# Zero products of TensorE in the idle spots of a planned attention-and-mixer kernel, with one PSUM bank less for the first batch

## The chip, the cores and the metric

The kernel runs on one core of a Trainium2 chip. The metric is the device time of one execution in microseconds (us). The engines are TensorE (PE in the profile; its weight loads are PEld), VectorE (DVE), ScalarE (ACT), GpSimd (POOL) and SyncE (SP). PE multiplies from SBUF into PSUM, which has eight banks of 512 float32 columns per partition; DVE and ACT read PSUM and work on SBUF.

## The reference

Block-sparse attention over 4 batches, 8 heads, 768 tokens and head size 64, followed by a residual mixer. Every query block of 32 tokens sees its neighbours, the first and the last block, and three sampled ones:

```python
scores = q @ k.T / sqrt(D);  scores = where(mask, scores, -1e9)
attn = softmax(scores);      x = attn @ v            # heads side by side: (4, 768, 512)
a1 = alpha1 * x + beta1
u = x + lam * einsum('ts,bsd->btd', w_tok, a1)       # tokens are mixed
a2 = alpha2 * u + beta2
out = u + lam * (relu(a2 @ w_ch1) @ w_ch2)           # channels, 512 -> 2048 -> 512
```

Inputs and output are float32; the kernel multiplies in bfloat16 and float16.

## The kernel before

Heads are handled in 16 pairs, four pairs to a batch, and each pair in 9 units of 1024 score columns. A unit is a scores job on PE (line 658, or 736 for the later pairs, into one of two PSUM tiles "sps"), an exponential on ACT (line 673 or 762, into one of 11 SBUF tiles "eT"), for the later pairs a masking on DVE (line 767), and a P·V job on PE (line 698, function `single`, for pairs 0 to 5; line 794, function `pv_of`, for the others). The P·V jobs of one head accumulate over four and a half units (or nine half ones) in one PSUM bank; behind the last, `norms` takes the reciprocal of the row sums (line 630) and multiplies (line 633), which frees the bank. When a pair is normalised, DVE prepares its tokens (lines 850, 858), PE multiplies by w_tok (line 870), DVE adds and scales (880, 886), and a transpose (907, for the first batch) brings it to the layout that the channel products want. When all four pairs of a batch are there, the first channel product (line 943) makes 16 tiles for each half batch, which ACT or DVE turn by relu into "hts" (954, 958), and the second (line 988) multiplies these by w2b into a bank "cp" or, late, "ops".

PSUM is full: two tiles "sps" of two banks each, two tiles "mm" of one bank (transposes, token products, first channel products), one bank "ops" and one bank "cp". For batch 0, when no second product exists yet, a head's P·V may take either "ops" or "cp" (line 712).

The order of the work is written by a planner at build time. Every piece of work is a `Job` with an engine, a duration in ns from simple formulas, a priority (a smaller tuple goes first), the jobs that it depends on, and the slots that it takes and gives back. A clock runs through events; whenever an engine is free by its own account, the ready job of the best priority whose slots are free is put next on that engine (from line 1088). Scores have priority 1, P·V and transposes 2, token products 3, and channel products 4 and 5. The jobs are emitted in this order, and `pin_order` (line 49) fixes it for each engine. On the chip nothing is timed: each engine runs its instructions in that order and waits for the semaphores that they need. `st["ch2"]` becomes true when the first second-product job takes "cp"; until then the planner has no channel product with w2b in hand. `pe_idle` lists the stretches in which PE, by the planner's clock, has nothing to do.

Loads are issued on POOL's queue in a fixed order, held back by the planner's estimate of the DMA's backlog and, for later pairs, by a flag that DVE raises at a chosen unit (lines 306, 324). SP's queue issues the stores of the output and the transposing DMAs of the later pairs.

Before the attention begins, products of a zeroed tile are issued on PE, nine of 512 columns and later seven of 128 columns:

```python
    warm = wk.tile([P, 512], BF, name="warm", tag="eT", bufs=NET)
    nc.vector.memset(warm[:], 0.0)
    wps = ps.tile([P, 512], FP, name="cp", tag="cp", bufs=1)

    def keep_warm(n, w):
        for _ in range(n):
            nc.tensor.matmul(wps[:, 0:w], warm[:, 0:P], warm[:, 0:w], start=True, stop=True)
```

They write the bank "cp", which nobody reads before it is overwritten. The tile "warm" is one of the ring of 11 "eT" tiles.

Of the kernel before, what the change touches and what calls it, by code (L numbers as in the profile page):

```python
# [13 lines left out]
BF = mybir.dt.bfloat16  # L14
# [13 lines left out]
P = 128  # L28
# [10 lines left out]
NET = 11  # L39
# [27 lines left out]
def kernel(  # L67
# [41 lines left out]
    pp = ctx.enter_context(tc.tile_pool(name="persist", bufs=1))  # L109
# [51 lines left out]
    for i in range(1, NQB):  # L161
        nc.sync.dma_start(kx[i][MB, :], ind_dr.ap())

    warm = wk.tile([P, 512], BF, name="warm", tag="eT", bufs=NET)
    nc.vector.memset(warm[:], 0.0)
    wps = ps.tile([P, 512], FP, name="cp", tag="cp", bufs=1)

# [475 lines left out]
    def single(p):  # L643
        b, n = pairs[p]
        nonlocal last_pv
        prev_pv = None
        for u in range(NU):
            i = p * NU + u

            def qk(p=p, u=u):  # L650
                sps = ps.tile([P, UN], FP, name="sps", tag="sps", bufs=2)
                f = u * UN
                while f < (u + 1) * UN:
                    a, r = divmod(f, NT * S)
                    jt, c = divmod(r, S)
                    w = min(S - c, 512 - f % 512)
                    h = (2 * p + a) % NQB
                    nc.tensor.matmul(  # L658
                        sps[:, f - u * UN : f - u * UN + w],
                        kx[h][0:KC, ts(jt, P)],  # L660
                        qx[h][0:KC, c : c + w],
                        start=True,
                        stop=True,
                    )
                    f += w
                tl["sps", p, u] = sps
                st["qk"] += 1

            def ex(p=p, u=u):
                eT = wk.tile([P, UN], F16, name="eT", tag="eT", bufs=NET)  # L670
                sps = tl.pop(("sps", p, u))
                for c in (slice(0, 512), slice(512, UN)) if (p, u) == (0, 0) else (slice(0, UN),):
                    nc.scalar.activation(eT[:, c], sps[:, c], AF.Exp, bias=EXPB, scale=SCALE)  # L673
                eTs[p, u] = eT

            hs = {divmod(u * UN, NT * S)[0], divmod((u + 1) * UN - 1, NT * S)[0]}
            deps = [head_ready[2 * p + a] for a in hs]
            if i:
                deps.append(qk_jobs[i - 1])
            give = ("head",) if u in (NU // 2, NU - 1) else ()  # L680
            jq = Job("PE", mmt(2, 512) + (8 if u % 3 != 1 else 8), (1, i), qk, deps, take=("sps",), give=give)
            jq.gate = i
            qk_jobs[i] = jq
            exp_jobs[i] = je = Job("ACT", 950.0, (1, i), ex, [jq], take=("eT",), give=("sps",), lat=160.0)

            lo, hi = u * GU, (u + 1) * GU
            segs = [(lo, hi)] if u != NU // 2 else [(lo, HT), (HT, hi)]
            for si, (s0, s1) in enumerate(segs):
                a = s0 // HT

                def pv(p=p, u=u, s0=s0, s1=s1, a=a):
                    if s0 % HT == 0:
                        tag = tl.pop(("opsel", p, a))
                        ops[p, a] = ps.tile([P, 512], FP, name=tag, tag=tag, bufs=1)
                    vx = vext[p % NV]
                    for i in range(s0, s1):
                        jt, t = divmod(i % HT, NT)
                        nc.tensor.matmul(  # L698
                            ops[p, a][:, t * VW : t * VW + D + 1],
                            eTs[p, u][:, ts(i - u * GU, P)],  # L700
                            vx[:, a, jt, 0 : D + 1],
                            start=(i % HT == 0),
                            stop=(jt == NT - 1),
                            skip_group_check=True,
                        )

                first = s0 % HT == 0
                deps = [je, putv[p]] + ([prev_pv] if prev_pv else [])
                give = ("eT",) if s1 == hi else ()
                if s1 == 2 * HT:  # L710
                    give += ("vext",)
                take = ((("ops", "cp") if b == 0 else ("ops",), ("opsel", p, a)),) if first else ()
                prev_pv = Job("PE", mmt(s1 - s0, D + 1), (2, i, si), pv, deps, take=take, give=give)
                last_pv = prev_pv
                if s1 % HT == 0:
                    pv_last[p, a] = prev_pv
                    norms(p, a)
# [358 lines left out]
    while left:  # L1076
        moved = True
        while moved:
            moved = False
            for e in free_at:  # L1080
                if free_at[e] > t:
                    continue
                best = None
                if e == "POOL" and dma_free[0] - t > AHEAD:
                    seq += 1
                    heapq.heappush(events, (dma_free[0] - AHEAD, -seq, None))
                    continue
                for r, j in by_eng[e]:
                    if r > t or j.done is not None:
                        continue  # L1090
                    if e == "POOL" and j is not loads[0]:
                        continue
                    key = (gated(j), j.prio)
                    if (best is None or key < best[0]) and can(j):
                        best = (key, j)
                if best is None:
                    continue
                j = best[1]
                can(j)
                for tk in j.take:  # L1100
                    if isinstance(tk, tuple):
                        o = chosen[tk[1]]
                        slots[o] -= 1
                        tl[tk[1]] = o
                        tl["slot", tk[1]] = o
                        if o == "cp" and tk[0][0] == "cp":
                            st["ch2"] = True
                    else:
                        slots[tk] -= 1
                j.out = j.fn(e) if len(j.eng) > 1 else j.fn()  # L1110
                if getattr(j, "ch", False):
                    st["ch"] += j.dur
                if e == "PE" and t - free_at[e] > 1:
                    pe_idle.append((free_at[e], t))
                dur = j.alt.get(e, j.dur)
                if getattr(j, "slow", False) and t < 85000.0:
                    dur = 2.2 * dur
                free_at[e] = t + dur
                lat = j.lat if j.lat is not None else DRAIN + SEM if e == "PE" else SEM
                j.done = t + dur + lat  # L1120
                if j.xfer is not None:
                    dma_free[0] = max(dma_free[0], t + 2300.0) + j.xfer
                    j.done = dma_free[0] + 200.0
                    loads.pop(0)
                seq += 1
                heapq.heappush(events, (j.done, seq, j))
                if e == "PE":
                    for s in succ.get(j.n, ()):
                        if s.eng == ("PE",):
                            early.add((j.n, s.n))  # L1130
                            waiting[s.n] -= 1
                            if not waiting[s.n]:
                                by_eng["PE"].append((t + dur, s))
                heapq.heappush(events, (free_at[e], -seq, None))
                for e2 in j.eng:
                    by_eng[e2] = [x for x in by_eng[e2] if x[1] is not j]
                left -= 1
                moved = True
        if not left:
            break  # L1140
        if not events:
            raise RuntimeError(f"stuck at {t}: " + str([(e, len(v)) for e, v in by_eng.items()]) + str(slots))
        t = max(t, events[0][0])
        while events and events[0][0] <= t:
            _, _, j = heapq.heappop(events)
            if j is None:
                continue
            for g in j.give:
                if isinstance(g, tuple):
                    slots[tl.pop(("slot", g))] += 1  # L1150
                else:
                    slots[g] += 1
            for s in succ.get(j.n, ()):
                if (j.n, s.n) in early:
                    continue
                waiting[s.n] -= 1
                if not waiting[s.n]:
                    for e in s.eng:
                        by_eng[e].append((t, s))
# [31 lines left out]
```

## Time and profile before

| | us |
|---|---|
| median of 4 runs | 324.66 |
| lowest and highest | 323.75 and 325.54 |
| profiled execution | 323.75 |
| its span, first to last instruction | 322.0 |
| PE busy | 308.3 |
| DVE busy | 208.9 |
| ACT busy | 206.3 |
| POOL busy | 49.7 |

The mean granted clock of PE over the span is 0.995 of full speed. Busy time of PE counts a product from its start to the end of its drain, and products overlap, so a busy PE isn't PE at its peak. A line such as "L698 MATMUL ops<-vext,eT ... x8" is a group of eight products of line 698 that write the tile ops from vext and eT. In a timeline a row gives the start and the length of such a group, and in brackets how long the engine was idle before it and which instruction's end released it.

### The profile page before, as it was taken

The numbers are of one execution on the slowest core, as the hardware profiler recorded it, in microseconds if no ns is written. First come the engines' busy times: TensorE is split into PE (matmuls) and PEld (weight loads), VectorE is DVE, ScalarE is ACT, GpSimd is POOL, SyncE is SP. The second block draws the span as 40 slices with busy tenths as digits, with TensorE's granted clock in tenths as the row PEclk, the third lists the DMA queues.
The fourth block names the chain that finished last, engine by engine and source line by source line (L and its number), as shares of the span: only waits on it lengthen the run. The fifth ranks groups of instructions, "written<-read, shape, count | busy, mean of one in ns | idle before, by whom it ended". The sixth has DMA issues, their size and how long they took to land.

```text
span 322.0 us, 7616 instructions
## 1 busy us (share of the span) xinstructions
PE 308.3 (96%) x3238; PEld 189.5 (59%) x3238; DVE 208.9 (65%) x416; ACT 206.3 (64%) x262; POOL 49.7 (15%) x77
## 2 busy tenths in 40 slices
PE   7879989899999999999899999999999999999996
PEld 3666868666655465555555455555655565555544
DVE  4559876878987797878778677687778660201001
ACT  4999997897885665746684584756784526354530
POOL 4647132200303030202103030030000000000000
PEclk9999998999999999999999999999999999999999
DMA  6999999996556654073815527064010201201102
GB/s 147 191 236 210 211 239 175 255 156 79 70 79 113 101 101 83 33 126 90 122 26 100 115 53 130 35 105 109 3 26 35 68 24 25 100 0 50 50 22 76
DMA packets 46774, 31.95 MB, mean 99 GB/s; under 512 B 27516, under 2 KB 42264, under 8 KB 46612
## 3 DMA queue, kind: packets, MB, share of 16 engines
q0 software_dynamic: 16496, 17.83, 32.9%
q1 hardware_dynamic: 29992, 13.40, 18.5%
q8 instruction: 25, 0.41, 0.6%
q10 hardware_dynamic: 252, 0.24, 0.3%
q14 instruction: 9, 0.07, 0.1%
HBM read 32.04 MB, written 7.47 MB: 123 GB/s over the span
## 4 chain that ended last, share of the span: by engine, by line
PE 67%; ACT 10%; DVE 7%; issue 6%; DMA 5%; POOL 3%; POOLq 0%; ACTq 0%
PE cp L988 19%; PE mm L943 18%; ACT eT L673 7%; PE ops L794 6%; PE mm L870 6%; PE sps L736 5%; DMA k<-in_k_dram 4%; PE ops L988 4%; PE sps L658 3%; PE sps L943 2%; ACT kx L270 2%; PE ops L698 2%; DMA v<-in_v_dram 2%; PE cp L170 1%; DVE x_sb L880 1%
## 5 line engine op out<-in xcount | busy, mean ns | idle before, releaser
L762 ACT ACTIVATE eT<-sps 128x1024 f16<-128x1024 f32 x90 | 88.1, 1021 | 33.8 <-PE sps L736 32.2
L943 PE MATMUL mm<-uT,w1b 128*128 128x384 bf16 x472 | 90.9, 326 | 0.9 <-DVE x_sb L880 0.5
L954 ACT ACTIVATE hts<-mm,b1t 128x384 bf16<-128x384 f32 x89 | 51.8, 582 | 57.7 <-PE mm L943 55.5
L988 PE MATMUL cp<-w2b,hts 128*128 128x512 bf16 (+1 forms) x336 | 80.1, 374 | 0.7 <-DVE ot L1005 0.7
L943 PEld LDWEIGHTS <-w1b 128*128 128x128 bf16 x512 | 46.7, 97 | 33.4 <-issue 5.0
L767 DVE TENSOR_TENSOR eT<-eT,maskT 128x1024 f16<-128x1024 f16 x90 | 60.6, 685 | 7.7 <-ACT eT L762 7.5
L988 PEld LDWEIGHTS <-hts 128*128 128x128 bf16 x400 | 36.6, 98 | 35.8 <-issue 2.9
L673 ACT ACTIVATE eT<-sps 128x1024 f16<-128x1024 f32 (+1 forms) x55 | 52.6, 1015 | 5.5 <-PE sps L658 5.1
L1005 DVE TENSOR_TENSOR ot<-x_sb,cp 128x512 f32<-128x512 f32 (+1 forms) x21 | 14.1, 672 | 46.2 <-PE cp L988 45.8
L794 PEld LDWEIGHTS <-eT 128*128 128x128 f16 x720 | 29.5, 97 | 18.4 <-DVE eT L767 7.0
L870 PE MATMUL mm<-a1p,wtokT 128*128 128x128 bf16 x576 | 37.1, 221 | 0.1
L794 PE MATMUL ops<-vext,eT 128*128 128x65 f16 x720 | 35.5, 194 | 1.5 <-DVE eT L767 1.5
L658 PE MATMUL sps<-qx,kx 88*128 88x512 bf16 (+1 forms) x144 | 31.7, 329 | 5.3 <-ACT eT L673 4.2
L870 PEld LDWEIGHTS <-wtokT 128*128 128x128 bf16 x576 | 33.6, 99 | 2.5 <-issue 0.5
L736 PE MATMUL sps<-qx,kx 64*128 64x512 bf16 (+1 forms) x240 | 27.3, 326 | 0.0
L306 POOL COPY held<-flag 1x1 bf16<-1x1 bf16 x8 | 5.9, 740 | 131.1 <-DVE flag L324 131.1
L958 DVE TENSOR_SCALAR hts<-mm,b1t 128x384 bf16<-128x384 f32 x29 | 17.8, 615 | 10.7 <-PE mm L943 10.5
L698 PEld LDWEIGHTS <-eT 128*128 128x128 f16 x432 | 19.7, 99 | 5.7 <-issue 0.5
L880 DVE TENSOR_TENSOR x_sb<-x_sb,mm 128x384 f32<-128x384 f32 x32 | 17.6, 550 | 7.3 <-PE mm L870 7.3
L658 PEld LDWEIGHTS <-kx 88*128 88x128 bf16 x144 | 12.8, 98 | 11.4 <-issue 7.0
L886 DVE TENSOR_TENSOR ub<-x_sb,a_bc 128x384 bf16<-128x384 f32 x32 | 17.2, 552 | 0.3
L736 PEld LDWEIGHTS <-kx 64*128 64x128 bf16 x240 | 8.2, 94 | 15.4 <-issue 12.9
(76 smaller groups left out, 238.3 us busy)
## 6 DMA issues: line engine op xcount, KB each, us to landing
out_dram<-ot SPq DMA_DIRECT2D x23, 256.0 KB, 2.0
v<-in_v_dram POOLq DMA_DIRECT2D x16, 192.0 KB, 5.8
q<-in_q_dram POOLq DMA_DIRECT2D x15, 192.0 KB, 3.7
k<-in_k_dram POOLq DMA_DIRECT2D x15, 192.0 KB, 5.1
w1b<-in_moe_w_ch_dram POOLq DMA_DIRECT2D x4, 512.0 KB, 9.9
w2b<-in_moe_w_ch_dram POOLq DMA_DIRECT2D x4, 512.0 KB, 14.9
wtk<-in_moe_w_tok_dram POOLq DMA_DIRECT2D x3, 384.0 KB, 9.7
mask_rows<-maskT POOLq DMA_DIRECT2D x1, 1152.0 KB, 12.8
```

The source lines that it names most:

```text
L658: nc.tensor.matmul(sps[:, f - u * UN : f - u * UN + w], kx[h][0:KC, ts(jt, P)], qx[h][0:KC, c : c + w], start=True, stop=True,)
L673: nc.scalar.activation(eT[:, c], sps[:, c], AF.Exp, bias=EXPB, scale=SCALE)
L698: nc.tensor.matmul(ops[p, a][:, t * VW : t * VW + D + 1], eTs[p, u][:, ts(i - u * GU, P)], vx[:, a, jt, 0 : D + 1], start=(i % HT == 0), s ...
L736: nc.tensor.matmul(sps[:, a * 512 + lo : a * 512 + lo + w], kx[sl][r, ts(jt, P)], qx[sl][r, c : c + w], start=True, stop=True,)
L762: nc.scalar.activation(eT[:], sps[:], AF.Exp, bias=EXPB, scale=SCALE)
L767: nc.vector.tensor_tensor(out=e, in0=e, in1=maskT[:, u, :].unsqueeze(1).broadcast_to([P, 2, 512]), op=ALU.min,)
L794: nc.tensor.matmul(ops[p, a][:, t * VW : t * VW + D + 1], eTs[p, u][:, a * 512 + c * P : a * 512 + (c + 1) * P], vx[:, a, jt, 0 : D + 1], ...
L870: nc.tensor.matmul(tp[:, j, :], wtokT[:, s, ts(3 * g + j, P)], tl["a1p", p][:, s, :], start=(s == 0), stop=(s == NT - 1),)
L880: nc.vector.tensor_tensor(out=sl, in0=sl, in1=tl.pop(("tp", p, g))[:], op=ALU.add)
L943: nc.tensor.matmul(hp[:, 0:HS], w1b[:, dk, ts(f, P)], uTs[b][:, dk, ts(hf, HS)], start=(dk == 0), stop=(dk == 3),)
L954: nc.scalar.activation(hts[kk][:, f, :], hp[:, 0:HS], AF.Relu, bias=b1t[:, f : f + 1], scale=1.0)
L988: nc.tensor.matmul(cps[kk, mi][:, 0:w], hts[kk][:, nk, ts(m, P)], w2tile[0][:, nk, lo : lo + w], start=(nk == 0), stop=(nk == 15),)
```

## The change

Three edits. The tile "warm" gets a buffer of its own, which lives as long as the kernel. The P·V jobs of batch 0 take the bank "ops" alone, as those of the later batches do. And when the planner puts a job on PE while `st["ch2"]` is false, it first emits zero products of 128 columns into the bank "cp": as many as fit into the stretch from PE's planned end of its last job to the start of this one, less 60 ns, at 56 ns each. They are emitted ahead of the job's instructions in PE's order; they take no time on the planner's clock, and nothing waits for them.

```diff
-    warm = wk.tile([P, 512], BF, name="warm", tag="eT", bufs=NET)
+    warm = pp.tile([P, 512], BF, name="warm", tag="warm")
...
-                take = ((("ops", "cp") if b == 0 else ("ops",), ("opsel", p, a)),) if first else ()
+                take = ((("ops",), ("opsel", p, a)),) if first else ()
...
-                j.out = j.fn(e) if len(j.eng) > 1 else j.fn()
                 if getattr(j, "ch", False):
                     st["ch"] += j.dur
+                if e == "PE" and not st["ch2"]:
+                    keep_warm(int((t - free_at[e] - 60.0) / 56.0), P)
+                j.out = j.fn(e) if len(j.eng) > 1 else j.fn()
                 if e == "PE" and t - free_at[e] > 1:
                     pe_idle.append((free_at[e], t))
```

## The prediction

> **What bounds the kernel now.** I read the page first, then busy time by stretch, then the chain of waits and the timeline of the place that they point to. From the page:
>
> ```profile
> PE 308.3 (96%) x3238; PEld 189.5 (59%) x3238; DVE 208.9 (65%) x416; ACT 206.3 (64%) x262; POOL 49.7 (15%) x77
> PE   7879989899999999999899999999999999999996
> ACT  4999997897885665746684584756784526354530
> PEclk9999998999999999999999999999999999999999
> ```
>
> PE is the bound over the whole, but a slice is 8 us, and in the first six or seven ACT is as full as PE while PE has holes. In that stage ACT's exponentials (1015 ns each, line 673) set the pace and PE waits for them; from about 65 us PE is full and sets the end. The only slice whose granted clock is not 9 is the seventh. By stretch (columns: stretch; PE, PEld, DVE, ACT, POOL busy us and count; clock; DMA share; GB/s):
>
> ```profile
> 40.00:44.00 4.00, 3.70 (x70) 3.05 (x68) 3.45 (x7) 3.80 (x5) 3.34 (x5) 1.00 1.27 198
> 44.00:48.00 4.00, 3.10 (x53) 2.50 (x50) 2.42 (x8) 3.95 (x5) 0.00 (x0) 0.86 1.23 274
> 48.00:52.00 4.00, 4.00 (x52) 3.46 (x51) 1.81 (x5) 2.60 (x4) 0.00 (x0) 0.71 1.04 214
> 52.00:56.00 4.00, 4.00 (x77) 3.23 (x75) 3.19 (x8) 3.29 (x5) 1.74 (x3) 1.00 0.87 138
> ```
>
> The clock was granted 0.86 of 4 us and then 0.71 of 4 us. If it was one stretch at half speed, it lasted (0.14 + 0.29) x 4 / 0.5 = 3.4 us; asked alone, 46.8 to 50.3 shows 0.51, so it does. In it ACT, full until then, is busy for 2.60 us of 4: it waits for a slowed PE. What came ahead of it, from PE's timeline (start, length, instruction; in brackets the idle time and who ended it):
>
> ```profile
> 42.87 0.50 PE L212 MATMUL mm<-identb,rel 128*128 128x128 bf16 x6
> 43.67 0.54 PE L454 MATMUL mm<-be2b,w1b 128*128 128x1 bf16 x16 [0.30 <-ACT uT L270]
> 44.59 0.59 PE L658 MATMUL sps<-qx,kx 88*128 88x512 bf16 x3 [0.39 <-ACT eT L673]
> 45.02 0.41 PE L698 MATMUL ops<-vext,eT 128*128 128x65 f16 x8
> 45.41 0.54 PE L454 MATMUL mm<-be2b,w1b 128*128 128x1 bf16 x16
> 46.46 0.64 PE L658 MATMUL sps<-qx,kx 88*128 88x512 bf16 x2 [0.51 <-ACT eT L673]
> ```
>
> Here stand three idle times, and two groups of one-column products that hardly use the array. The printed idle begins when the last product has drained; PE could have issued some 0.14 us earlier (163 ns of a product less the 25 ns between starts, (0.54 - 0.163)/15), so the room at 44.59 is about 0.39 + 0.14 = 0.53 us.
>
> **The change, part by part.**
>
> *Zero products.* How many come in is a count that the code makes: (gap - 60)/56 in each idle spot of the planner's list. For the order of the kernel before, the list holds 119 products in 23 spots up to the first product with w2b (76 us in the trace); the new order will differ somewhat. The duration: the early zero products in the timeline are
>
> ```profile
> 6.25 0.56 PE L170 MATMUL cp<-warm 128*128 128x128 bf16 x7
> ```
>
> so (0.56 - 0.219)/6 = 57 ns from start to start (219 ns is the shortest in the answer on the cp tile). 119 x 57 ns = 6.8 us of issue. They wait for nothing, so what matters is whether each lot fits in the real hole. Worked from starts in the timeline, PE's real holes between 8 and 65 us come to some 9.7 us, and they lie where the planner has them: 9 products (0.51 us) for 0.53 at 44.59; 9 (0.51 us) for 0.51 + 0.14 = 0.65 at 46.46; 17 (0.97 us) for about 0.94 at 58.62. Three lots don't fit: 8 products (0.45 us) ahead of a transpose at 17.54 where there is no hole, 8 (0.45 us) for 0.29 at 32.18, and 7 (0.39 us) ahead of the transpose at 63.65. Behind each lies the next hole (0.52 us at 18.40, 0.22 at 35.53, 0.43 in two holes by 64.43) that PE would have waited out anyway, and this covers the delay. Without that cover the misfits cost 1.07 us in all. I take 0.2 us, range 0 to 1.1. The next job's weight load, which the trace has inside the hole, now follows the zero products; it overlaps the last of them, and its cost is within the 0.2. Two instructions per product add 238 to 7616; the instruction queue carries 0.41 MB in all, 3% more of it is nothing here. No DMA, no POOL or SP instruction is added or moved past.
>
> *The clock.* In the two holes and the one ahead of the first one-column group (3 products) the plan puts 21 products, 1.2 us, in the 3.4 us before the dip. Do zero products count as activity? The answer on the cp tile has the 512-wide zero products at a median of 620 ns against 379 ns for the same width at line 988, and the clock reads 1.00 from 5.9 us on, after nothing but zeros and a handful of small products: so they do. A rule weighs against this. The Trainium skill, "TensorE: Matmul & The Clock Gate", Part 1 and "Why this matters for your kernels", has the clock halved after an idle window of about 3.4 us and advises no gap over some 3 us. The longest idle time here is 0.78 us, so by that rule there is nothing to be dropped and nothing to gain: the sum would be +0.6 us. The row shows a dip of just that length after a sparse, not idle, window, and the row decides. But the same section has the window running freely, not tied to the kernel's start, which no single run can show; then an execution whose windows cut the sparse stretch in two may have no dip, and I keep that as a rival. Value of the dip: at most 3.41 x 0.5 = 1.7 us (PE's lost issue), at least 0 (if the waits behind swallow it). I take the engine that sets the pace in that place, ACT, which lost 4.00 - 2.60 = 1.4 us: -1.4 us.
>
> *One bank less for the first batch.* Heads 1, 3, 5 and 7 of the first batch accumulate in cp, the others in ops. With ops alone, the first P·V job of a head waits for reciprocal and multiply (197 + 557 ns, lines 630 and 633) of the head before. The trace has this already where the second batch begins:
>
> ```profile
> 63.53 0.28 PE L698 MATMUL ops<-vext,eT 128*128 128x65 f16 x4
> 63.65 0.76 PE L907 MATMUL mm<-identb,ub 128*128 128x128 bf16 x6
> 64.43 0.59 PE L658 MATMUL sps<-qx,kx 88*128 88x256 bf16 x3
> 64.86 0.77 PE L698 MATMUL ops<-vext,eT 128*128 128x65 f16 x20
> ```
>
> From 63.65, the last issue of a head, to 64.86 are 1.2 us in which P·V stands still and other work goes on; then it catches up, 20 at a stretch. Behind a waiting P·V job only later P·V jobs queue in the plan, since scores have priority; ACT feels nothing until its 11 eT buffers fill, and 1.2 us is about one exponential. There are seven such turns in the first batch. For the turns near 14, 19, 26, 30 and 42 us a hole of the ACT-bound stage follows, and P·V that was put off goes into it. Those near 36 and 51 us fall in stretches without a hole, where token products (18 x 56 ns) and scores are ready to go first. Only the last head's end leads on: its normalisation at 55.9 to 56.9 us feeds the token product at 59.3, then the first channel product. Bounds: -0.5 (another order may also be luckier) to 7 x 1.2 = 8.4 us if every turn were bare. I take a third of one turn, 0.4 us, by the row above, where other work filled it.
>
> *The warm buffer.* It leaves the eT ring, where it was released by 7 us, and takes 1 KB per partition of its own: 0. What would cover it, the ring of 11, loses nothing.
>
> The sum, against the profiled execution: 323.75 - 1.4 + 0.2 + 0.4 = 322.95 us. That execution (span 322.0 and 1.75 around it) is the fastest of the four shown, 0.91 below their median, so the median to expect is 323.86, say **323.9 us**.
>
> **Rivals.**
>
> *No dip to save* (chance 0.19). The clock dip belongs to the profiled execution and not to the usual one, because the windows fall otherwise. Then +0.6 us stays: 325.3, less if the holes cover the 0.6: 324.7 to 325.3. For it speaks that the execution with the dip is the fastest of four; against it that the sparse stretch from 43.2 to 46.9 is longer than a window.
>
> *The re-sorted plan is worse: slower than before* (0.28). Its one mechanism is the late hand-over from the first batch to the second. P·V is put off in the full stretches at 36 and 51 us and is not made up before the last head's normalisation; then token product, transpose and first channel product come late, and PE, with nothing else ready at 59 to 64 us, idles or issues zeros. Each turn that is not made up costs its 1.2 us less the 0.3 us of one P·V job that was late anyway, 0.9 us. Four of the seven turns (from 30 us on) bare: 3.6 us, with the dip saved or not 325.7 to 328.2; the likeliest here 327. It decides from about 3 us, which outweighs the 1.4 gained and passes 326.3. For it: the page's PE row is 9 in those slices. Against it: the second batch lives with one bank, and the chain of waits names line 633 for only 0.2 us at line 698 and 1.0 us at line 794.
>
> *More than one dip in the usual execution* (0.15). The median lies 0.9 us above the profiled execution; if that is a second dip, the zeros save both: 324.66 - 2.8 + 0.6 = 322.5.
>
> **How the numbers follow.** The likeliest has 0.38, with a range of its own of 322.7 to 325.2 (dip worth 0 to 1.7, misfits to 1.1). All four runs before lie within 0.6%, so 0.5%, 1.6 us, is about what can be told from no change. Faster (under 323.0): the third rival's 0.15 and 0.07 of the likeliest, 0.22. Slower (over 326.3): the re-sorted plan's 0.28 and 0.03 of the others, 0.31. Same: 0.47. The range over the cases: 322.0 to 327.2.
>
> **What the new profile would show.** Right: the row by stretch has 1.00 at 44 to 52 us, ACT is near 4 of 4 there, line 170 has some 130 to 150 products instead of 16, idle times of line 658 from ACT shrink to nearly nothing, and no wait of over 1 us for line 633 stands before 65 us. The first channel product (66.2 us, line 943) comes about 1 us earlier. Wrong: the dip is there again, or elsewhere; or line 943 begins later than 66.2; or the dense part, which should be 255.8 us from there to the end as before, has another length, which would be the order and not the clock.

## The result and the profile after

The changed kernel took 322.21 us (median of 43 runs, 320.73 to 325.67) against 324.3 us for the kernel before (64 runs, 322.32 to 328.01): a ratio of 0.9941, 95% interval 0.9928 to 0.9955. It is 0.6% faster, where the likeliest forecast was 323.9 and "same". (The ratio, here and below, leaves out slow executions, those over 1.5% above the fastest of their kernel, and is not the quotient of the medians.) Its profiled execution has a span of 319.2 us against 322.0. From its page, with the rows shown of before:

```profile
PE 310.4 (97%) x3340; PEld 193.8 (61%) x3340; DVE 206.4 (65%) x411; ACT 208.5 (65%) x267; POOL 48.1 (15%) x77
PE   7999999999999999999899999999999999999996
ACT  4999989897775678756676577746665526254630
PEclk9999999999999999999999999999999999999999
```

PE's holes in the second, third, sixth and eighth slice are filled, and the clock's dip in the seventh is gone. By stretch, with the same columns as before:

```profile
40.00:44.00 4.00, 3.66 (x57) 3.01 (x54) 2.75 (x8) 3.06 (x5) 3.81 (x5) 1.00 1.28 197
44.00:48.00 4.00, 3.83 (x91) 3.33 (x89) 3.28 (x9) 3.98 (x5) 0.02 (x1) 1.00 1.19 272
48.00:52.00 4.00, 4.00 (x72) 3.59 (x69) 3.63 (x11) 3.80 (x5) 0.00 (x0) 1.00 1.00 191
```

ACT is busy for 3.80 of the 4 us from 48 us on (2.60 before). So far the forecast's picture holds. PE's timeline of the place, start and length of each group, shows the zero products (line 170) between the jobs:

```profile
44.64 0.54 PE L454 MATMUL mm<-be2b,w1b 128*128 128x1 bf16 x16
45.04 0.72 PE L170 MATMUL cp<-warm 128*128 128x128 bf16 x10
45.92 0.54 PE L454 MATMUL mm<-be2b,w1b 128*128 128x1 bf16 x16 [0.17 <-DVE kx L272]
46.32 0.27 PE L170 MATMUL cp<-warm 128*128 128x128 bf16 x2
46.43 0.60 PE L658 MATMUL sps<-qx,kx 88*128 88x512 bf16 x2
```

But the first channel product (line 943) begins at 65.5 us instead of 66.2, 0.7 us earlier, and the span is 2.8 us shorter: from there to the end are 253.7 us instead of 255.8. The first start of line 943, before and changed:

```profile
L943 PE MATMUL mm<-uT,w1b x472: 322/326/337, 66.2 to 308.1; 128*128 128x384 bf16 x158
L943 PE MATMUL mm<-uT,w1b x472: 322/326/337, 65.5 to 305.3; 128*128 128x384 bf16 x158
```

In that part neither kernel has zero products or a dip. The prediction had named this sign: another length of the dense part "would be the order and not the clock". One pair of executions is not much for 2 us, but the profiled executions of the experiments below say the same: 253.6 to 255.4 us in nine executions of the new order, 255.8 to 256.3 in three of the old one (and 253.9 in the old one once its late loads are let go, as the last experiment tells).

To see where the time went I set the start of each group of token products (line 870) against its start in the planner's own list; the difference is the lag of the chip behind the plan. The plan's end of PE is 0.75 us earlier in the new order (313.20 against 313.95; these are the planner's figures, not measurements). The lags in us, from the profiled executions (the last three columns are experiments told below):

| token group of | before | changed | bank only, first run | zeros, old order | loads not held |
|---|---|---|---|---|---|
| pair 0, first half | 0.94 | 1.13 | 1.07 | 1.15 | 1.08 |
| pair 3, second half | 2.95 | 1.69 | 2.95 | 1.73 | 2.98 |
| pair 9, second half | 2.25 | 1.76 | 2.59 | 0.71 | 2.14 |
| pair 10, first half | 3.43 | 2.68 | 3.39 | 1.67 | 3.74 |
| pair 11, first half | 4.26 | 2.59 | 3.30 | 2.11 | 3.74 |
| pair 12, first half | 5.13 | 2.74 | 3.63 | 4.38 | 3.56 |
| pair 15, second half | 4.77 | 2.74 | 3.88 | 4.01 | 3.19 |

The span's 2.8 us are thus 0.75 of plan and 2.03 of lag. Of the lag 1.26 is won by pair 3 (the dip), but by pair 9 the kernel before has caught up to within 0.49. Most of the rest comes where it falls back from 3.43 to 5.13 between pairs 10 and 12. The order of PE's jobs differs in 383 of 624 places, from 13 us of the plan to 252; the last 60 us are alike.

Each column is one execution, and the level changes between executions: three of the changed kernel have 2.74, 5.99 and 5.53 in the last row. The growth from pair 10 to pair 12 is what holds. It is 1.70, 2.71 and 2.67 us in three executions of the old order (before, zeros in the old order, and bank of pairs 0 and 1 taken away), and -0.10 to 0.95 us in the nine of the new order (1.26 with twice the zero products).

### The profile page after: what moved, and what is told of

Its sections match the earlier page's. It is cut to its first block, busy times and chain, and to the rows that moved or that the text cites. A ratio compares the mean times of both kernels' runs of the same rounds, so it can differ in the third digit from the quotient of the medians.

```text
span 319.2 us, 7815 instructions
## 1 busy us (share of the span) xinstructions
PE 310.4 (97%) x3340; PEld 193.8 (61%) x3340; DVE 206.4 (65%) x411; ACT 208.5 (65%) x267; POOL 48.1 (15%) x77
## 4 chain that ended last, share of the span: by engine, by line
PE 70%; DMA 14%; DVE 6%; issue 4%; ACT 3%; POOL 3%; POOLq 0%
PE cp L988 20%; PE mm L943 20%; PE ops L794 7%; PE sps L736 6%; DMA q<-in_q_dram 6%; PE mm L870 5%; PE ops L988 4%; DMA mask_rows<-maskT 4%; DMA v<-in_v_dram 3%; PE sps L658 3%; PE cp L170 2%; PE sps L943 2%; DMA k<-in_k_dram 2%; DVE eT L767 1%; DVE hts L958 1%
## 5 line engine op out<-in xcount | busy, mean ns | idle before, releaser
L954 ACT ACTIVATE hts<-mm,b1t 128x384 bf16<-128x384 f32 x96 | 55.9, 582 | 50.8 <-PE mm L943 48.4
L794 PEld LDWEIGHTS <-eT 128*128 128x128 f16 x720 | 29.2, 97 | 17.8 <-issue 4.2
L794 PE MATMUL ops<-vext,eT 128*128 128x65 f16 x720 | 34.8, 194 | 0.3 <-DVE eT L767 0.3
L306 POOL COPY held<-flag 1x1 bf16<-1x1 bf16 x8 | 4.3, 541 | 128.7 <-DVE flag L324 128.7
L698 PEld LDWEIGHTS <-eT 128*128 128x128 f16 x432 | 18.6, 97 | 4.5 <-DVE x_sb L633 0.4
L698 PE MATMUL ops<-vext,eT 128*128 128x65 f16 x432 | 20.5, 193 | 0.0
L958 DVE TENSOR_SCALAR hts<-mm,b1t 128x384 bf16<-128x384 f32 x22 | 13.5, 615 | 8.2 <-PE mm L943 8.2
L633 DVE TENSOR_TENSOR x_sb<-ops,rcp 128x384 f32<-128x384 f32 x32 | 17.8, 557 | 1.1
```

Of the source, the lines that this page charges most:

```text
L633: nc.vector.tensor_tensor(out=x_sb[:, s0 : s0 + NT, h * D : (h + 1) * D], in0=op[:, :, 0:D], in1=rcp[:].unsqueeze(2).broadcast_to([P, NT, D]),
L698: nc.tensor.matmul(ops[p, a][:, t * VW : t * VW + D + 1], eTs[p, u][:, ts(i - u * GU, P)], vx[:, a, jt, 0 : D + 1], start=(i % HT == 0), s ...
L794: nc.tensor.matmul(ops[p, a][:, t * VW : t * VW + D + 1], eTs[p, u][:, a * 512 + c * P : a * 512 + (c + 1) * P], vx[:, a, jt, 0 : D + 1], ...
L954: nc.scalar.activation(hts[kk][:, f, :], hp[:, 0:HS], AF.Relu, bias=b1t[:, f : f + 1], scale=1.0)
```

## The experiments

Two theories. **C**, mine: the clock carries the gain, through the zero products. **O**, its rival: the one bank re-sorts the plan, and the new order carries it. Kernels of one group ran on one chip and share its runs of the kernel before: 323.95 us for the first four, 324.18 for the next, 324.89 for the last.

### The bank without the zero products, and the zero products without the bank

The bank alone (the edits of buffer and bank stay):

```diff
-                if e == "PE" and not st["ch2"]:
-                    keep_warm(int((t - free_at[e] - 60.0) / 56.0), P)
```

> The changed kernel's order, with its one bank and its own warm buffer, but without the zero products in the idle spots. Theory C (the clock carries the gain): the zero products are what helps; this one keeps the dips and the price of the bank, +0.4 us over the kernel before: 324.3 to 325.2, granted clock at or under 0.995 in most executions. Theory O (the re-sorted order carries the gain): 322.2 to 323.2, with dips in it; in executions with clock 1.00 as fast as the changed kernel.

Measured: 322.0 us, ratio 0.9939 (0.9917 to 0.9962), just under the range of theory O: the changed kernel's gain whole, without one zero product in an idle spot. Its profiled execution has the dip as the kernel before has it, and a span of 320.3 us all the same:

```profile
44.00:48.00 4.00, 3.26 (x68) 2.51 (x66) 3.28 (x9) 4.00 (x5) 0.69 (x1) 0.87 1.24 217
48.00:52.00 4.00, 4.00 (x53) 3.36 (x52) 2.52 (x7) 2.94 (x5) 0.00 (x0) 0.71 1.07 271
```

The zero products alone, in the kernel before with both banks, wherever cp is free in the plan (the warm tile has its own buffer here too, and `keep_warm` is told which tile to write):

```diff
+                if e == "PE" and not st["ch2"] and slots["cp"] > 0:
+                    n0 = int((t - free_at[e] - 60.0) / 56.0)
+                    if n0 > 0:
+                        wps = ps.tile([P, 512], FP, name="cp", tag="cp", bufs=1)
+                        keep_warm(n0, P, wps)
                 j.out = j.fn(e) if len(j.eng) > 1 else j.fn()
```

> The order of the kernel before, both banks for the first batch, and zero products by the same formula wherever cp is free in the plan: 79 of the 119, among them the 21 of the sparse stretch at 43 to 47 us. Theory C: the clock stays at 1.00 and the time falls by 1.2 to 2 us, to 322.3 to 323.1. Theory O: under 0.8 us of gain, 323.5 to 324.6, since the order is the old one; it can gain only as often as the kernel before has a dip.

Measured: 323.89 us, ratio 0.9996 (0.9973 to 1.0018): no gain that can be told. In the profiled execution the dip is gone:

```profile
44.00:48.00 4.00, 4.00 (x76) 3.29 (x73) 2.75 (x9) 3.95 (x5) 0.00 (x0) 1.00 1.21 285
48.00:52.00 4.00, 4.00 (x69) 3.47 (x68) 3.09 (x8) 3.44 (x5) 0.00 (x0) 1.00 0.96 186
```

So the zero products do to the clock what was forecast, and still don't bring time on the median; the order does. C falls as the cause of the gain. The lag table shows where the saving went in this execution: by pair 9 it is 1.54 us ahead of the kernel before, by pair 12 only 0.75, since it falls back further between pairs 10 and 12. Over all executions, the 14 without a dip have a median of 323.20 us and the 8 with one 326.70. Why those with a dip take so long is not shown.

### Twice the zero products

```diff
-                    keep_warm(int((t - free_at[e] - 60.0) / 56.0), P)
+                    keep_warm(2 * int((t - free_at[e] - 60.0) / 56.0), P)
```

> The changed kernel with twice the zero products in every idle spot: 102 more at 57 ns, 5.8 us of issue. If the spots of the chip are as the plan has them, the second half is bare wherever PE, not ACT, is late next. Both theories: slower than the changed kernel, by at most 5.8 us, by some 2 to 4 us since ACT's pace hides a part (324.2 to 326.2). If it costs under 0.5 us, the misfits of the single lot (1.07 us if bare) are worth nothing.

Measured: 327.28 us, ratio 1.0084 (1.0051 to 1.0118), 5.1 us above the changed kernel of the same chip (322.21), past the 2 to 4 us that were expected. Six of the nine executions have a dip; the three without one have a median of 325.11 us, which is 3.0 us above the changed kernel's executions without a dip. In the profiled one, 72 of the 102 added products, 4.1 us of issue, stand ahead of the first token group, which lags by 3.14 us instead of 1.14. So by then about half of what was added has come through as delay, and the other half went into waiting time that was there anyway.

### The changed kernel beside these

> The changed kernel, unaltered, beside the three others on the same chip: 322.2 by both theories, clock 1.00 in most executions; its executions with a dip, if there are any, should be 1.4 to 1.7 us longer than those without.

Measured: 322.21 us, ratio 0.9946 (0.9925 to 0.9967). Three of 22 executions have a dip, and they are 2.6 us longer than the others (324.71 against 322.11), not 1.4 to 1.7. Its profiled execution (span 322.5) is one with a dip, and shows what came first. From the timeline of PE, and by stretch:

```profile
52.98 0.23 PE L698 MATMUL ops<-vext,eT 128*128 128x65 f16 x2
55.15 0.58 PE L698 MATMUL ops<-vext,eT 128*128 128x65 f16 x14 [1.94 <-issue]
```

```profile
52.00:56.00 4.00, 2.06 (x45) 1.71 (x43) 1.65 (x3) 2.62 (x3) 0.57 (x2) 1.00 0.86 140
56.00:60.00 4.00, 4.00 (x56) 2.94 (x53) 3.19 (x9) 2.17 (x3) 3.55 (x5) 0.68 0.96 291
```

PE stood still for 1.94 us inside a group of P·V products, waiting for nothing that the profile shows, and 2.2 us later the clock fell. In this execution the dip follows a stop of PE, so the difference between executions with and without a dip is not the dip's price alone.

### Which turn of the bank matters

The planner's list says that taking the second bank from pair 2 alone already gives the new order from 51 us on. Only line 712 differs from the kernel before (and the warm tile has its own buffer in both):

```diff
-                take = ((("ops", "cp") if b == 0 else ("ops",), ("opsel", p, a)),) if first else ()
+                take = ((("ops", "cp") if b == 0 and p != 2 else ("ops",), ("opsel", p, a)),) if first else ()
```

> The kernel before, its warm tile in a buffer of its own, no zero products in idle spots, and the second bank taken away from pair 2 alone (heads 4 and 5, planned at 29 to 41 us); pairs 0, 1 and 3 keep both. By the planner's list every job from 51 us on then stands as in the changed kernel. Theory O (one turn that is made to wait re-sorts all that follows, and this is the gain): as fast as the bank-only kernel, 321.7 to 322.6. Rival B (the bank as such, in all its turns, matters): about a quarter of the gain, 323.3 to 323.8.

Measured: 322.54 us, ratio 0.9942 (0.9912 to 0.9971). And with `b == 0 and p >= 2` in that place:

> The same, but the bank is taken from pairs 0 and 1 alone; the planner's list then differs from that of the kernel before in 10 of 624 PE jobs, all before 31 us. Theory O: no gain, 323.6 to 324.3. Rival B: half of the gain, 322.7 to 323.3.

Measured: 324.05 us, ratio 0.9999 (0.9979 to 1.002). It is not the number of turns: pair 2 is enough for the whole gain, and pairs 0 and 1 bring none (pair 3 alone was not run). In the planner's list the first difference that pair 2 makes is at 35 us, the turn from head 4 to head 5. In the kernel before (first fence) the four P·V products of head 5 go to cp at once; with pair 2 on one bank (second fence) they stand behind the token products, a scores job, a transpose and another scores job:

```profile
35.97 0.53 PE L698 MATMUL ops<-vext,eT 128*128 128x65 f16 x12
36.33 0.28 PE L698 MATMUL cp<-vext,eT 128*128 128x65 f16 x4
36.45 1.17 PE L870 MATMUL mm<-a1p,wtokT 128*128 128x128 bf16 x18
37.46 1.03 PE L658 MATMUL sps<-qx,kx 88*128 88x512 bf16 x5
```

```profile
36.34 1.17 PE L870 MATMUL mm<-a1p,wtokT 128*128 128x128 bf16 x18
37.35 0.60 PE L658 MATMUL sps<-qx,kx 88*128 88x512 bf16 x2
37.78 0.50 PE L907 MATMUL mm<-identb,ub 128*128 128x128 bf16 x6
38.12 0.60 PE L658 MATMUL sps<-qx,kx 88*128 88x256 bf16 x3
38.55 0.62 PE L698 MATMUL ops<-vext,eT 128*128 128x65 f16 x15
```

P·V stands still from 36.34 to 38.55 us while other work goes on, and then does 15 products at a stretch. Hardly any time is lost or won by it: at the end of pair 3 the lag is 3.21 us, against 2.95 in the kernel before. But the list that follows is another one, and it is the faster one.

### Fewer zero products, and the three side by side

Zero products only in spots planned between 40 and 47.5 us, 19 of the 102:

```diff
-                if e == "PE" and not st["ch2"]:
+                if e == "PE" and 40000.0 < t < 47500.0:
```

> The changed kernel's order, with zero products only in spots planned between 40 and 47.5 us, 19 of its 102, where the kernel before has its dip. If the zeros elsewhere cost what the dip's absence gains: 321.2 to 321.8, the best so far, clock 1.00 in most executions. If zeros are worth nothing by either sign: 322.0 to 322.3.

Measured: 321.27 us, ratio 0.9885 (0.9841 to 0.993), no dip in any of 6 executions. Beside it:

> The bank-only kernel once more, on the chip of the others, since its first six executions leave open what the zero products add to the new order. If the dips cost it time as they do the kernel before (1.0 us between executions with and without one): 322.3 to 322.8 over all, 321.9 without a dip and 322.9 with one. If a dip costs nothing in this order: 322.0 in both.

Measured: 321.44 us, ratio 0.9899 (0.9864 to 0.9933), faster than either case expected; 321.36 without a dip and 321.76 with one. These two kernels can't be told apart, so the three kernels ran once more on one chip:

> The changed kernel, unaltered, on one chip with the next two, since the earlier comparisons of it with the bank-only kernel were on one chip and those with the few zeros on another: 321.9 to 322.4. If the zeros outside the sparse stretch cost nothing, it is level with the next two.

> The changed kernel's order with the 19 zero products planned between 40 and 47.5 us alone. If the other 83 zero products cost what the traces leave open (0.4 to 0.6 us): 321.2 to 321.7, under the changed kernel. If not: level with it, 321.9 to 322.4.

> The bank-only kernel, no zero products in idle spots. If dips cost little in this order: 321.4 to 321.9, level with the 19 zero products. If the dips cost as in the kernel before, 0.3 to 0.8 us above the kernel with 19.

Measured: 322.68 us for the changed kernel, ratio 0.9954 (0.9917 to 0.9991); 321.58 with 19 zero products, 0.9908 (0.9879 to 0.9937); 322.38 with the bank alone, 0.9937 (0.9912 to 0.9961). With all runs of the result and the study taken together the medians are 322.30, 321.56 and 322.12. All three intervals against the kernel before overlap. The medians of twelve runs each put the kernel with 19 zero products 1.1 us under the changed kernel (95% interval from resampled medians 0.5 to 2.2 us) and 0.8 us under the bank alone (0.3 to 1.1). So on this chip the 19 zero products are worth something in the new order, and the other 83 give it back; on the chip before, the difference from the bank alone was 0.2 us, within the noise. Not all of it can be the clock: the five executions of the bank alone without a dip have a median of 322.22 us here, still 0.6 us above. What else the 19 products do is open. This version has the lowest median of the three.

How often the mean granted clock was under 0.997, and the medians without and with it, by executions of the result and the study:

| kernel | share with a dip | median without | median with |
|---|---|---|---|
| before | 80 of 113 | 323.32 | 324.69 |
| bank only | 12 of 26 | 321.69 | 322.31 |
| changed | 10 of 78 | 322.17 | 324.69 |
| 19 zero products | 0 of 18 | 321.56 | |

The medians mix three chips. Taken chip by chip, executions with a dip are longer than those without by 1.0, 1.4 and 1.9 us for the kernel before, and by -0.1, 0.4 and 0.2 us for the bank alone (groups of 2 to 7 executions), where a dip thus costs little. In the changed kernel, of the same order, the ten with a dip are far longer; the one of them that was profiled had the stop of PE ahead of its dip. All the zero products together make dips rare, but the dips that are left are not cheap; in the kernel with the old order and zero products, 8 of 22 executions had one.

### The loads of two pairs let go

What made the old order slow between pairs 10 and 12? Its trace has two waits of PE there, on DVE instructions (waits of PE from 170 to 200 us):

```profile
PE cp L988 <- DVE ot L1005: 0.7, 1, 0.7
PE mm L943 <- DVE x_sb L880: 0.5, 1, 0.5
PE ops L794 <- DVE eT L767: 0.2, 1, 0.2
```

And ahead of these, in DVE's timeline, casts of loads that hadn't landed, with the instructions that PE wants queued behind them:

```profile
177.93 0.36 DVE L508 COPY rel<-k 128x768 bf16<-128x768 bf16 x1 [1.26 <-DMA k<-in_k_dram]
178.48 0.36 DVE L816 COPY vext<-v 128x768 f16<-128x768 f16 x1 [0.18 <-DMA v<-in_v_dram]
178.75 0.68 DVE L1005 TENSOR_TENSOR ot<-x_sb,cp 128x512 f32<-128x512 f32 x1
...
193.99 0.36 DVE L508 COPY rel<-q 128x768 bf16<-128x768 bf16 x1 [2.11 <-DMA q<-in_q_dram]
194.26 0.68 DVE L767 TENSOR_TENSOR eT<-eT,maskT 128x1024 f16<-128x1024 f16 x1
```

To take this cause alone, I left the order of the kernel before as it is and let the loads of pairs 13 and 14 go as soon as their buffers are free:

```diff
-                1300.0 if p < 2 else 980.0, prio, deps, take=("ld",), held=p if deps else None,
+                1300.0 if p < 2 else 980.0, prio, deps, take=("ld",), held=p if deps and p not in (13, 14) else None,
```

> The kernel before, its order by the planner unaltered, without the POOL copy that holds the loads of pairs 13 and 14 back until DVE's flag; they go out as soon as their buffers are free. If the late landings of these loads, which stop DVE's casts and with them the engine's later work, make PE's waits at 179.5 and 195 us: these waits are gone or under 0.3 us, and the time falls by 0.8 to 1.5 us, to 322.6 to 323.3. If the waits are not the loads' doing, or the loads now collide with others: 323.8 to 324.5, or slower.

Measured: 322.46 us, ratio 0.9945 (0.991 to 0.9979), a little better than the forecast range. No wait of PE is left from 170 to 200 us, and DVE's queue goes through:

```profile
176.58 0.35 DVE L508 COPY rel<-k 128x768 bf16<-128x768 bf16 x1
176.85 0.35 DVE L816 COPY vext<-v 128x768 f16<-128x768 f16 x1
177.87 0.69 DVE L1005 TENSOR_TENSOR ot<-x_sb,cp 128x512 f32<-128x512 f32 x1 [0.66 <-PE cp L988]
...
191.28 0.35 DVE L508 COPY rel<-q 128x768 bf16<-128x768 bf16 x1
```

In the table above its lag stays at 3.74 and 3.56 where the kernel before goes to 4.26 and 5.13. The old order with the loads of two pairs released is as fast as the changed kernel, with its dip in place (11 of 12 executions). The profiled execution's 1.6 us less span is just the lag's 1.58.

So the late loads are what the old order lost between pairs 10 and 12. In the new order the casts still wait for loads from 170 to 200 us, 2.8 us in the changed kernel against 3.8 before, but they stand elsewhere in DVE's queue, and PE waits for DVE for 0.3 us there against 1.4. That the new order gains by this is read from the traces alone. The new order with these loads let go was not run, so whether the two gains would add is open.

## Why the prediction was right or wrong, step by step

- **PE's holes and the zero products: right on where they lie, too low on their cost.** The changed plan has 102 of them, 118 products at line 170 with the first sixteen, where I had expected 130 to 150. They lie in the holes, and by the first token group cost about 0.1 to 0.2 us (lag 1.13 against 0.94 to 1.07). That all of them together cost 0.2 us is too low: the 83 outside the sparse stretch cost about 1 us on the one chip where this was compared. Where this time goes after 32 us no single trace shows.
- **The clock, -1.4 us: right in the profiled pair, wrong on the median.** The dip is gone and by pair 3 the lag is 1.26 us less. But zeros in the old order gained nothing on the median, 0.9996. The rule as I read it from the Trainium skill's "TensorE: Matmul & The Clock Gate" (Part 1), by which there was nothing to be dropped, does not hold here: five kernels show the dip at this place with no idle time over 0.8 us in the 4 us ahead of it, so choosing the row was right. The mistake was to take what ACT lost at the dip for what the execution loses at its end. My lower bound, 0 "if the waits behind swallow it", is nearer: in the profiled execution with zeros in the old order, the late loads took back half of what had been won by pair 9. The rival that the dip may belong to some executions only was half right: 80 of 113 have it. The rival of a second dip was wrong as the usual case: 66 of the 113 have a mean clock of 0.993 to 0.995, as the profiled execution with its one dip, and only 14 have 0.990 or less.
- **The bank, +0.4 us: wrong in size and sign, and this is the step that failed.** "I take a third of one turn, 0.4 us". With the bank alone there is a gain of 1.95 us (322.0 against 323.95). How a turn goes was well read: at 36 us P·V stands still for 2.2 us and catches up, as at 63.5 us. What I set at 0.5 us and called "luckier" was the main effect. I had even said of the turn near 36 us that token products and scores would go first, and took it for a reason that nothing changes; it is the turn that re-sorts the list behind it.
- **The re-sorted plan as a rival for the slow side: right mechanism, wrong sign and place.** A new order did decide, but not in the hand-over at 59 to 64 us, where bank only and before lag alike (2.95). It decided mostly at 170 to 200 us, where the old order has PE wait behind late loads in DVE's queue. The plan's own 0.75 us may add to it; no run takes that part alone.
- **"Same" as the likeliest: wrong by a little**; the range of 322.0 to 327.2 holds 322.21, near its end. That is luck: its low end stood for dearer or more dips, and not for a faster order.

## What to carry to other kernels

Where an order is written by a planner, cost an edit of its slots or priorities by what it does to the list, not only by the wait that it adds: list both orders' first difference, and look what comes after. A priced wait at one place can be nothing while the list behind it is worth 0.6%. The planner's list alone doesn't show it all: the late loads were found by setting the chip's starts against it. And before filling holes of PE, compare several executions with and without the clock's dip on one chip, and try filling only the stretch ahead of the dip.

## What the runs showed of the hardware that I had not expected

- A drop of the granted clock to 0.5 for 3.4 us came without any idle time of PE over 0.8 us: the 3.4 us ahead of it held 32 one-column products and three short holes. Ten zero products of 128 columns at 45 us, with nine elsewhere nearby, kept the mean clock at 0.999 or above in 18 of 18 executions; without them it was under 0.997 in 12 of 26 in the same order.
- PE can stop for 1.94 us in the middle of a group, with no semaphore that the profile shows (one profiled execution in three of the changed kernel). What stops it is open; it was not tried.
- DVE's queue passes a late load on to PE: casts that waited 1.26 and 2.11 us for a landing cost PE 0.7 and 0.5 us of visible idle time. Letting six loads go early has a price too, which is smaller: PE's wait behind the cast of pair 12's k, at 159 us, grew from 0.94 to 1.36 us.
